# A gated linear-attention kernel on one core: V in three column chunks that carry the router and gate columns, V before K, and a new order of the q stage

## The chip, the cores and the metric

One core of one Trainium2 chip runs the kernel. The metric is device time of one execution in microseconds (us); lower is better. TensorE does the matrix products, VectorE (DVE) and ScalarE (ACT) work on vectors and read the matmul results from PSUM, GpSimd (POOL) works on SBUF alone, and SyncE (SP) issues most transfers. Each engine executes its own queue in order; semaphores order them against each other.

## The reference

The input `x` has 2048 tokens of 1024 numbers (bf16). With 32 heads of 32 columns:

```python
g = sigmoid((x * gate_w).sum(-1, keepdims=True))
q, k, v = heads of x @ wqkv
pq, pk  = q @ w_phi, k @ w_phi                       # per head, 32 x 32
phi     = concat(softmax(p), softmax(-p))            # for q and for k
kv, z   = sum_s phi_k^T v, sum_s phi_k               # per head: 64 x 32 and 64
a       = (phi_q @ kv) / (phi_q . z + 1e-6) @ wo
r       = x @ w_r ; the one token with the largest r goes through a gated FFN (1024 -> 3584 -> 1024)
b       = x + (FFN output * sigmoid(r)) at that token
out     = g * a + (1 - g) * b
```

## The kernel before

**Staging.** The tokens are 16 tiles of 128. `xT_tile(t)` transposes a loaded tile on TensorE into `pT`, and VectorE (even tiles) or ScalarE (odd tiles) copies it to `xT`; it also takes the tile's squared norm on ScalarE (`nx2`, for a range check at the end) and, on VectorE, two products with broadcast rows that give the router value and the gate logit of each token (`rg`). The weights of q and k are folded with `w_phi`: `fold(which, wf, kb)` multiplies a transposed block of `wqkv` (`wT`, loaded by transposing DMAs) with the block-diagonal `BDm`, casts the result on VectorE and takes its squared norm there (`nw2`).

**K and V.** A unit is a tile and a half of the columns (512). `k_v(t, hf)` makes a unit of V with eight matmuls and ScalarE writes it to `v_all`. `k_s0(u)` makes a unit of k features: eight matmuls, two exponentials on ScalarE (`e`), a sum and a reciprocal on VectorE, a product on GpSimd (`phi`). `k_kv(u)`, LAG = 3 iterations behind, adds the products of phi and v into `kvps`, a PSUM region of three banks. The source order is: four tiles' transposes and V, the folds of k with four more tiles, and then one loop that mixes `k_kv`, V units by a running count, `k_s0`, the remaining transposes, the route (`gates_and_route`: the largest router value, its index, the chosen token's column), FFN chunks (1 MB of weights each, two buffers) and the folds of q. The count `nv` starts at 12 when 16 units are done, so units 12 to 15 are made a second time.

**q stage.** `kv_finish` copies kvps to `KV`. `q_front(sb, j)` makes 128 feature columns for 512 tokens (eight matmuls, two exponentials into `E`; 32 in all). `q_num(t, hf)` multiplies a tile's half of the features with `KV` into the PSUM tile `num`, of which there is one buffer; VectorE then runs a chain of seven instructions that ends in `T`, and GpSimd adds the two halves of `T` to `o_sb`. `q_oT(t)` transposes the tile's o by DMA (the last tile on TensorE) and ScalarE makes `xg` from x; `q_wo(t, nh)` multiplies with half of `wo`, VectorE makes the output, SyncE stores it. The loop runs q_num eight iterations behind q_front (NL = 8), q_oT and q_wo two and three behind q_num.

**Order.** A scheduler of the framework takes the program in source order as priority and lets a ready instruction pass one whose inputs or buffer are not there yet by its own reckoning; the order on each engine is then fixed.

**PSUM.** V and K results and q fronts share two buffers (`psA`), transposes, folds and wo results share two others (`psB`).

Of the kernel before, what the change touches and what calls it, by code (L numbers as in the profile page):

```python
# [160 lines left out]
def kernel(  # L161
# [22 lines left out]
    wraw = kscope.enter_context(tc.tile_pool(name="wraw", bufs=2))  # L184
    xs = kscope.enter_context(tc.tile_pool(name="xs", bufs=4))
# [22 lines left out]
    v_all = kpool.tile([P, NU, HH, DH + 1], BF, name="v_all")  # L208
# [36 lines left out]
    wv_sb = wraw.tile([P, KB, D], BF, name="wv_sb", tag="w16")  # L245
    xload(0)
    nc.sync.dma_start(out=wv_sb[:, :, 0:512], in_=w_v[:, :, 2 * D:2 * D + 512])
    for t in range(1, 4):
        xload(t)
    nc.sync.dma_start(out=wv_sb[:, :, 512:D], in_=w_v[:, :, 2 * D + 512:3 * D])  # L250
# [19 lines left out]
    def wT_load(which, kb):  # L270
        if kb == 0:
            wT[which] = wraw.tile([P, KB, D], BF, name="wT", tag="w16")
        nc.sync.dma_start_transpose(out=wT[which][:, :, kb * P:(kb + 1) * P],
                                    in_=A_wqkv[kb * P:(kb + 1) * P, (1 - which) * D:(2 - which) * D])

    def fold(which, wf, kb):
        for jh in range(2):
            pW = psB.tile([P, 4, P], F32, name="pW", tag="pB")
# [8 lines left out]

    def gates_and_route():
# [13 lines left out]
        gw_rows = const.tile([KB, P], BF, name="gw_rows")  # L302
        nc.scalar.dma_start(out=gw_rows[:], in_=gate_w.rearrange("(kb p) -> kb p", p=P))
        gw_ps = m1_ps[:, 0:4].bitcast(BF)
        nc.tensor.transpose(out=gw_ps, in_=gw_rows[:], identity=ident[0:KB, 0:KB])
        nc.vector.tensor_copy(out=gw_sel[:], in_=gw_ps)
# [110 lines left out]
    def k_kv(u):  # L417
        t, hf = divmod(u, 2)
        phi = kst.pop(u)
        for pl in range(NPU):  # L420
# [3 lines left out]
                             rhs=v_all[:, u, 2 * pl:2 * pl + 2, :].rearrange("p h d -> p (h d)"),  # L424
# [104 lines left out]
    for kb in range(KB):  # L529
        wT_load(0, kb)  # L530
    for t in range(4):
        xT_tile(t)
    for t in range(4):
        k_v(t, 0)
    for t in range(4, 8):
        xload(t)
    xT_tile(4)
    for t in range(4):
        k_v(t, 1)
    VL = 12  # L540
    for kb in range(KB):
        fold(0, wkf, kb)
        if kb % 2 == 1:
            xT_tile(5 + kb // 2)
            xload(8 + kb // 2)
# [96 lines left out]
```

## Time and profile before

| | |
|---|---|
| time, median of 3 runs | 354.42 us (353.15 to 354.64) |
| the profiled execution, time | 353.82 us |
| its span, first to last instruction | 352.0 us |
| mean granted TensorE clock | 0.975 of 2.4 GHz |
| busy: TensorE, weight loads, VectorE, ScalarE, GpSimd | 296.9, 161.0, 246.1, 137.4, 115.5 us |
| moved by DMA | 47.98 MB |

Busy time is the sum of an engine's records. A matmul's record also holds the time in which its last results drain while the next one already runs, so the distance between two starts is what a matmul takes of TensorE in a full stretch. Idle time counts only on the path that sets the end.

### The profile page before, as it was taken

The numbers are of one execution on the slowest core, as the hardware profiler recorded it, in microseconds if no ns is written. First come the engines' busy times: TensorE is split into PE (matmuls) and PEld (weight loads), VectorE is DVE, ScalarE is ACT, GpSimd is POOL, SyncE is SP. The second block draws the span as 40 slices with busy tenths as digits, with TensorE's granted clock in tenths as the row PEclk, the third lists the DMA queues.
The fourth block names the chain that finished last, engine by engine and source line by source line (L and its number), as shares of the span: only waits on it lengthen the run. The fifth ranks groups of instructions, "written<-read, shape, count | busy, mean of one in ns | idle before, by whom it ended". The sixth has DMA issues, their size and how long they took to land. (4 is left out here: it accounts for less than half of the span.)

```text
span 352.0 us, 6368 instructions
## 1 busy us (share of the span) xinstructions
PE 296.9 (84%) x2478; PEld 161.0 (46%) x2518; DVE 246.1 (70%) x501; ACT 137.4 (39%) x230; POOL 115.5 (33%) x81
## 2 busy tenths in 40 slices
PE   1398979879779999999998999969999999847590
PEld 0334545435334555655555465535555555423340
DVE  4623999999968435599994237866777777766740
ACT  2434434865524343433343555233343344311110
POOL 5000000355564645456555012331233223321411
PEclk9999999999989999999999999999999999987987
DMA  6999812940000435453465997792344344342201
GB/s 209 281 199 323 289 53 62 177 124 27 2 0 0 122 121 170 149 162 116 128 182 180 312 345 236 211 212 60 92 113 97 91 114 110 89 107 61 60 31 36
DMA packets 64818, 47.98 MB, mean 136 GB/s; under 512 B 35344, under 2 KB 55824, under 8 KB 64784
## 3 DMA queue, kind: packets, MB, share of 16 engines
q1 hardware_dynamic: 63360, 46.94, 47.8%
q10 hardware_dynamic: 1392, 0.59, 0.7%
q8 instruction: 21, 0.34, 0.4%
q14 instruction: 13, 0.11, 0.1%
q0 software_dynamic: 32, 0.00, 0.0%
HBM read 35.19 MB, written 4.20 MB: 112 GB/s over the span
## 5 line engine op out<-in xcount | busy, mean ns | idle before, releaser
L413 POOL TENSOR_TENSOR phi<-e,rs 128x1024 bf16<-128x1024 bf16 x32 | 68.7, 2151 | 114.4 <-DVE rs L411 90.5
L499 POOL TENSOR_TENSOR o_sb<-T 128x512 bf16<-128x512 f32 x32 | 40.6, 1267 | 108.2 <-DVE T L495 108.2
L523 PE MATMUL po<-wo_sb,oT 128*128 128x512 bf16 x249 | 63.0, 394 | 10.7 <-DMA oT<-o_sb 10.3
L391 PE MATMUL pv<-wv_sb,xT 128*128 128x512 bf16 x278 | 69.5, 388 | 0.5
L402 PE MATMUL pk<-wkf,xT 128*128 128x512 bf16 x245 | 62.0, 383 | 0.6
L459 PE MATMUL pq<-xT,wqf 128*128 128x512 bf16 x244 | 59.8, 379 | 0.9 <-ACT E L462 0.3
L265 DVE SCALAR_TENSOR_TENSOR junk<-xs_t,wr_bc 128x1024 bf16<-128x1024 bf16 x32 | 42.8, 1364 | 13.6 <-DMA xs_t<-in_A_x_dram 13.6
L409 DVE TENSOR_REDUCE ssum<-e 128x32 f32<-128x1024 bf16 x32 | 38.7, 1208 | 17.1 <-ACT e L406 17.1
L523 PEld LDWEIGHTS <-oT 128*128 128x128 bf16 x256 | 25.1, 101 | 40.8 <-DMA oT<-o_sb 11.7
L495 DVE TENSOR_TENSOR T<-num,ab 128x1024 f32<-128x1024 f32 x32 | 39.2, 1225 | 3.5 <-DVE ab L493 0.5
L461 ACT ACTIVATE E<-pq 128x512 bf16<-128x512 f32 x32 | 19.1, 596 | 53.0 <-PE pq L459 43.0
L393 ACT CAST v_all<-pv 128x512 bf16<-128x512 f32 x36 | 21.2, 588 | 47.5 <-PE pv L391 47.5
L391 PEld LDWEIGHTS <-xT 128*128 128x128 bf16 x288 | 27.0, 100 | 27.9 <-issue 2.2
L525 DVE SCALAR_TENSOR_TENSOR o_out<-po,gate,xg 128x512 bf16<-128x512 f32 x32 | 23.8, 745 | 22.0 <-PE po L523 22.0
L402 PEld LDWEIGHTS <-xT 128*128 128x128 bf16 x256 | 24.1, 98 | 26.5 <-issue 1.3
L459 PEld LDWEIGHTS <-wqf 128*128 128x128 bf16 x256 | 23.5, 97 | 23.5 <-issue 0.6
L405 ACT ACTIVATE e<-pk 128x512 bf16<-128x512 f32 x32 | 19.1, 598 | 38.7 <-PE pk L402 38.6
L514 ACT ACTIVATE xg<-xin,omg 128x1024 f32<-128x1024 bf16 x16 | 18.4, 1148 | 39.1 <-DVE o_out L525 19.7
L480 PE MATMUL num<-KV,E 128*128 128x136 bf16 x256 | 21.1, 226 | 4.3 <-DVE T L495 4.2
L256 PE MATMUL pT<-ident,xs_t 128*128 128x128 bf16 x128 | 11.3, 242 | 15.2 <-DMA xs_t<-in_A_x_dram 11.7
L480 PEld LDWEIGHTS <-E 128*128 128x128 bf16 x256 | 17.1, 99 | 12.3 <-DVE T L495 7.2
L422 PE MATMUL kvps<-v_all,phi 128*128 128x66 bf16 x256 | 14.0, 194 | 8.9 <-POOL phi L413 8.8
(96 smaller groups left out, 281.0 us busy)
## 6 DMA issues: line engine op xcount, KB each, us to landing
wch<-in_B_w_gate_dram SPq DMA_DIRECT2D x7, 1024.0 KB, 5.3
wch<-in_B_w_up_dram SPq DMA_DIRECT2D x7, 1024.0 KB, 5.5
wchd<-in_B_w_down_dram SPq DMA_DIRECT2D x7, 1024.0 KB, 6.2
xs_t<-in_A_x_dram SPq DMA_DIRECT2D x16, 256.0 KB, 3.9
xin<-in_A_x_dram SPq DMA_DIRECT2D x16, 256.0 KB, 2.7
out_dram<-o_out SPq DMA_DIRECT2D x32, 128.0 KB, 1.9
wv_sb<-in_A_wqkv_dram SPq DMA_DIRECT2D x2, 1024.0 KB, 6.9
wo_sb<-in_A_wo_dram SPq DMA_DIRECT2D x1, 2048.0 KB, 11.4
```

The source lines that it names most:

```text
L265: nc.vector.scalar_tensor_tensor(out=junk2[:], in0=xt_[:], scalar=1.0, in1=wr_bc[:, c, :], op0=ALU.mult, op1=ALU.mult, accum_out=rg[:, c, ...
L391: nc.tensor.matmul(pvf, lhsT=xT[:, kb, t * P:(t + 1) * P], rhs=wv_sb[:, kb, hf * 512:(hf + 1) * 512], start=(kb == 0), stop=(kb == KB - 1))
L393: nc.scalar.copy(out=v_all[:, t * 2 + hf, :, 0:DH], in_=pv[:])
L402: nc.tensor.matmul(pkf, lhsT=xT[:, kb, t * P:(t + 1) * P], rhs=wkf[:, kb, hf * 512:(hf + 1) * 512], start=(kb == 0), stop=(kb == KB - 1))
L409: nc.vector.tensor_reduce(out=ssum[:], in_=e2, axis=AX.X, op=ALU.add)
L413: nc.gpsimd.tensor_tensor(out=phi[:].rearrange("p h s f -> p (h s) f"), in0=e2, in1=_bc(rs[:], [P, HH * 2, DH]), op=ALU.mult)
L459: nc.tensor.matmul(pq[:], lhsT=wqf[:, kb, j * P:(j + 1) * P], rhs=xT[:, kb, sb * SB:(sb + 1) * SB], start=(kb == 0), stop=(kb == KB - 1))
L480: nc.tensor.matmul(num[:, b * NSTR:b * NSTR + KVW], lhsT=E[:, j, sg, tl * P:(tl + 1) * P], rhs=KV[:, sg, j, :], start=True, stop=True)
L495: nc.vector.tensor_tensor(out=T[:].rearrange("p s (j h) d -> p (s j) h d", h=4), in0=nb[:, :, 0:128].rearrange("p b (h d) -> p b h d", d=D ...
L499: nc.gpsimd.tensor_tensor(out=st["o"][:, hf * HH:(hf + 1) * HH, :], in0=T[:, 0], in1=T[:, 1], op=ALU.add)
L523: nc.tensor.matmul(po[:], lhsT=st["oT"][:, kb, :], rhs=wo_sb[:, kb, sl], start=(kb == 0), stop=(kb == KB - 1))
L525: nc.vector.scalar_tensor_tensor(out=o_out[:], in0=po[:], scalar=gate[:, t:t + 1], in1=st["xg"][:, sl], op0=ALU.mult, op1=ALU.add)
```

## The change

V is made in three chunks of columns, 0 to 352, 352 to 704 and 704 to 1026; the last two columns are the router's and the gate's weights, put beside the V weights in SBUF (`rows_in`), so that the matmul gives `rg` and a small VectorE copy takes it out. The two broadcast rows and the products with them are gone. All transposed copies are VectorE's, all squared norms ScalarE's. All of V is made first, each unit once, with all 16 folds among tiles 6 to 15; then all of K, with LAG = 5, 14 FFN chunks, and every fourth phi product on VectorE. In the q stage q_num runs four iterations behind the fronts and takes four tiles' first halves, then their second halves; q_wo takes one half a step, at the earliest three steps behind its q_oT. The chain behind num reads part of its numbers from PSUM instead of from a copy. Buffer counts follow.

```diff
+VC = [0, 352, 704, 1026]
+VW = 1026
...
-    wraw = kscope.enter_context(tc.tile_pool(name="wraw", bufs=2))
-    xs = kscope.enter_context(tc.tile_pool(name="xs", bufs=4))
+    wraw = kscope.enter_context(tc.tile_pool(name="wraw", bufs=1))
+    xs = kscope.enter_context(tc.tile_pool(name="xs", bufs=6))
...
-        nc.scalar.dma_start(out=wr_bc[:, 0, :], in_=B_w_r.unsqueeze(0).to_broadcast([P, D]))
-        nc.scalar.dma_start(out=wr_bc[:, 1, :], in_=gate_w.unsqueeze(0).to_broadcast([P, D]))
+    nc.scalar.dma_start(out=rows[0:KB, :], in_=B_w_r.rearrange("(kb p) -> kb p", p=P))
+    nc.scalar.dma_start(out=rows[KB:2 * KB, :], in_=gate_w.rearrange("(kb p) -> kb p", p=P))
...
+    for c in range(3):
+        lo, hi = VC[c], min(VC[c + 1], D)
+        nc.sync.dma_start(out=wv_sb[:, :, lo:hi], in_=w_v[:, :, 2 * D + lo:2 * D + hi])
+        for t in ((1, 2, 3), (4, 5), ())[c]:
+            xload(t)
+    def rows_in():
+        rows_ps = m2_ps[:, 0:KB].bitcast(BF)
+        nc.tensor.transpose(out=rows_ps, in_=rows[:], identity=ident[0:2 * KB, 0:2 * KB])
+        nc.vector.tensor_copy(out=wv_sb[:, :, D:VW].rearrange("p k c -> p c k"),
+                              in_=rows_ps.rearrange("p (c k) -> p c k", c=2))
+        nc.vector.tensor_copy(out=gw_sel[:], in_=rows_ps[:, KB:2 * KB])
...
-        if t % 2 == 0:
-            nc.vector.tensor_copy(out=xT[:, :, t * P:(t + 1) * P], in_=pT[:])
-        else:
-            nc.scalar.copy(out=xT[:, :, t * P:(t + 1) * P], in_=pT[:])
+        nc.vector.tensor_copy(out=xT[:, :, t * P:(t + 1) * P], in_=pT[:])
+        xsq[t] = xt_
+    def x_norm(t):
...
         nc.scalar.activation(out=junk[:], in_=xt_[:], func=ACTF.Square, accum_out=nx2[:, t:t + 1])
-        for c in range(2):
-            junk2 = wk.tile([P, D], BF, name="junk2", tag="junk", bufs=3)
-            nc.vector.scalar_tensor_tensor(out=junk2[:], in0=xt_[:], scalar=1.0, in1=wr_bc[:, c, :],
-                                           op0=ALU.mult, op1=ALU.mult, accum_out=rg[:, c, t:t + 1])
...
-        if kb == 0:
-            wT[which] = wraw.tile([P, KB, D], BF, name="wT", tag="w16")
+        wT[which, kb] = wraw.tile([P, KB, P], BF, name="wT", tag="wT", bufs=6)
...
-        nc.vector.scalar_tensor_tensor(out=junk3[:], in0=wf[:, kb, :], scalar=1.0, in1=wf[:, kb, :],
-                                       op0=ALU.mult, op1=ALU.mult, accum_out=nw2[:, which, kb:kb + 1])
+        nc.scalar.activation(out=junk3[:], in_=wf[:, kb, :], func=ACTF.Square, accum_out=nw2[:, which, kb:kb + 1])
...
+    def k_v(t, c):
+        lo, hi = VC[c], VC[c + 1]
+        h0, h1 = lo // DH, min(hi, D) // DH
+        pv = psA.tile([P, 512], F32, name="pv", tag="pA")
...
+            nc.tensor.matmul(pv[:, 0:hi - lo], lhsT=xT[:, kb, t * P:(t + 1) * P], rhs=wv_sb[:, kb, lo:hi],
                              start=(kb == 0), stop=(kb == KB - 1))
+        if c == 2:
+            nc.vector.tensor_copy(out=rg[:, :, t], in_=pv[:, D - lo:VW - lo])
...
+        phi = wk.tile([P, HH, 2, DH], BF, name="phi", tag="phi", bufs=6)
+        eng = nc.vector if u % 4 == 3 else nc.gpsimd
+        eng.tensor_tensor(out=phi[:].rearrange("p h s f -> p (h s) f"), in0=e2,
...
+            st = {"o": qw.tile([P, H, DH], BF, name="o_sb", tag="o_sb", bufs=5)}
+            xin = qw.tile([P, D], BF, name="xin", tag="xin", bufs=6)
...
-        nc.vector.tensor_copy(out=ds[:], in_=nb[:, :, 128:136])
+        nc.vector.tensor_copy(out=ds[:], in_=nb[:, 4:8, 128:136])
...
+        nc.vector.tensor_tensor(out=pr[:], in0=nb[:, 0:4, 128:136], in1=ds[:], op=ALU.mult)
...
+    xT_tile(0)
+    rows_in()
+    k_v(0, 0)
+    for t in range(1, 4):
+        xT_tile(t)
+        k_v(t, 0)
+    for t in range(4):
+        k_v(t, 1)
+    xT_tile(4)
+    for t in range(4):
+        k_v(t, 2)
+        x_norm(t)
+        xload(t + 6)
+        wload(1)
+    for t in range(4, NT):
+        if t + 1 < NT:
+            xT_tile(t + 1)
+        if t + 6 < NT:
+            xload(t + 6)
+        if t < 6:
+            wload(1)
+        for c in range(3):
+            k_v(t, c)
+        x_norm(t)
+        for _ in range(0 if t < 6 else 2 if t < 12 else 1):
+            w, kb = fq.pop(0)
+            fold(w, wkf if w == 0 else wqf, kb)
+            wload(1)
+    gates_and_route()
+    LAG = 5
...
     for i in range(NU + LAG):
         if i >= LAG:
             k_kv(i - LAG)
...
+        if i >= 4 and i % 2 == 0 and ci < 14:
             ffn_chunk(ci)
...
-    NL = 8
+    NL = 4
+    WL = 4
...
         if 0 <= n < NU:
-            q_num(n // 2, n % 2)
+            sb, r = divmod(n, 8)
+            q_num(sb * 4 + r % 4, r // 4)
+        m = n - 1
+        if 0 <= m < NU and m % 8 >= 4:
+            t = (m // 8) * 4 + m % 4
+            q_oT(t)
+            wq_ += [(i + WL - 1, t, 0), (i + WL - 1, t, 1)]
...
+        if wq_ and (wq_[0][0] <= i):
+            _, t, nh = wq_.pop(0)
+            q_wo(t, nh)
```

## Rows read from the trace of the kernel before

**Rows 1.** Five stretches: length, busy us and instructions by engine, clock, DMA.

```profile
0.00:34.80 34.80, 19.75 (x105) 10.48 (x108) 15.56 (x27) 12.95 (x20) 5.27 (x16) 1.00 0.95 251
34.80:100.40 65.60, 54.18 (x396) 29.28 (x401) 65.14 (x102) 35.49 (x62) 18.73 (x7) 0.99 0.38 101
100.40:183.30 82.90, 81.01 (x847) 45.56 (x858) 59.31 (x88) 32.46 (x60) 44.36 (x22) 0.99 0.38 116
183.30:301.30 118.00, 111.75 (x973) 61.12 (x987) 77.47 (x215) 49.83 (x81) 34.82 (x26) 1.00 0.60 167
301.30:344.00 42.70, 30.21 (x167) 14.57 (x168) 28.10 (x70) 6.69 (x7) 11.38 (x9) 0.88 0.28 72
```

**Rows 2.** Timeline of TensorE, three stretches: start us, length, line, out<-in.

```profile
39.51 0.61 PE L281 MATMUL pW<-BDm,wT 128*128 128x128 bf16 x8
39.96 1.24 PE L391 MATMUL pv<-wv_sb,xT 128*128 128x512 bf16 x4
...
122.23 0.94 PE L356 MATMUL small_ps<-xsT,wch 128*128 128x1 bf16 x32
123.03 0.41 PE L422 MATMUL kvps<-v_all,phi 128*128 128x66 bf16 x8
123.29 1.89 PE L391 MATMUL pv<-wv_sb,xT 128*128 128x512 bf16 x7
...
251.98 0.64 PE L480 MATMUL num<-KV,E 128*128 128x136 bf16 x8
252.45 1.89 PE L459 MATMUL pq<-xT,wqf 128*128 128x512 bf16 x8
254.18 1.89 PE L523 MATMUL po<-wo_sb,oT 128*128 128x512 bf16 x8
```

**Rows 3.** Timeline of the first 35 us, then one of SyncE's waits.

```profile
5.96 1.31 SPq L242 DMA_DIRECT2D xs_t<-in_A_x_dram  x3
...
6.17 1.03 PE L256 MATMUL pT<-ident,xs_t 128*128 128x128 bf16 x8 [6.17 <-DMA xs_t<-in_A_x_dram]
...
17.45 8.83 PE L391 MATMUL pv<-wv_sb,xT 128*128 128x512 bf16 x32
...
31.50 0.58 SPq L575 DMA_DIRECT2D wo_sb<-in_A_wo_dram  x1
...
SPq L242 <- DMA wr_bc<-in_B_w_r_dram: 4.2, 1, 4.2
```

**Rows 4.** Groups of instructions by line: count, busy us, mean ns, idle before.

```profile
L413 POOL TENSOR_TENSOR phi<-e,rs 128x1024 bf16<-128x1024 bf16 x32 | 68.7, 2151 | 114.4 <-DVE rs L411 90.5 <-PE kvps L422 5.1 <-ACT v_all L393 4.9
L523 PE MATMUL po<-wo_sb,oT 128*128 128x512 bf16 x249 | 63.0, 394 | 10.7 <-DMA oT<-o_sb 10.3
...
L265 DVE SCALAR_TENSOR_TENSOR junk<-xs_t,wr_bc 128x1024 bf16<-128x1024 bf16 x32 | 42.8, 1364 | 13.6 <-DMA xs_t<-in_A_x_dram 13.6
...
L409 DVE TENSOR_REDUCE ssum<-e 128x32 f32<-128x1024 bf16 x32 | 38.7, 1208 | 17.1 <-ACT e L406 17.1
...
L393 ACT CAST v_all<-pv 128x512 bf16<-128x512 f32 x36 | 21.2, 588 | 47.5 <-PE pv L391 47.5
...
L262 ACT ACTIVATE junk<-xs_t 128x1024 bf16<-128x1024 bf16 x16 | 17.0, 1061 | 5.8 <-DMA gw_rows<-in_gate_w_dram 4.3 <-DMA xs_t<-in_A_x_dram 1.5
...
L283 DVE CAST wqf<-pW 128x512 bf16<-128x512 f32 x16 | 10.5, 671 | 2.6 <-PE pW L281 2.6
...
L262 ACT ACTIVATION_READ_ACCUMULATOR junk<-xs_t 128x1 f32 x16 | 3.1, 194 | 0.0
```

**Rows 5.** Timeline of TensorE behind the last q matmul.

```profile
316.75 1.11 PE L480 MATMUL num<-KV,E 128*128 128x136 bf16 x8
...
321.88 0.64 PE L480 MATMUL num<-KV,E 128*128 128x136 bf16 x8
...
329.73 0.65 PE L480 MATMUL num<-KV,E 128*128 128x136 bf16 x8 [0.67 <-DVE T L495]
333.25 0.65 PE L480 MATMUL num<-KV,E 128*128 128x136 bf16 x8 [2.87 <-DVE T L495]
```

More of the change, by code (lines that the diff above doesn't have):

```diff
@@ L207 @@
     wkf = kpool.tile([P, KB, D], BF, name="wkf")
-    v_all = kpool.tile([P, NU, HH, DH + 1], BF, name="v_all")
+    v_all = kpool.tile([P, NT, H, DH + 1], BF, name="v_all")
     KV = big.tile([P, 2, KB, KVW], BF, name="KV")
@@ L243, in xload @@
         xtiles[t] = xt_
-    wv_sb = wraw.tile([P, KB, D], BF, name="wv_sb", tag="w16")
+    wv_sb = wraw.tile([P, KB, VW], BF, name="wv_sb", tag="w16")
     xload(0)
[L247 to L250, printed above, removed]
+    for c in range(3):
[9 more added lines that the diff above has]
+        nc.vector.tensor_copy(out=gw_sel[:], in_=rows_ps[:, KB:2 * KB])
     def xT_tile(t):
@@ L301, in gates_and_route @@
         nc.sync.dma_start(out=r_row[0:1, :], in_=rT[:])
[L302 to L306, printed above, removed]
         mx8 = const.tile([1, 8], F32, name="mx8")
@@ L385, in moe_final @@
                             in_=y2[:], accum_op=ALU.add)
-    def k_v(t, hf):
-        pv = psA.tile([P, HH, DH], F32, name="pv", tag="pA")
-        pvf = pv[:].rearrange("p h f -> p (h f)")
+    def k_v(t, c):
+        lo, hi = VC[c], VC[c + 1]
+        h0, h1 = lo // DH, min(hi, D) // DH
+        pv = psA.tile([P, 512], F32, name="pv", tag="pA")
         for kb in range(KB):
-            nc.tensor.matmul(pvf, lhsT=xT[:, kb, t * P:(t + 1) * P], rhs=wv_sb[:, kb, hf * 512:(hf + 1) * 512],
+            nc.tensor.matmul(pv[:, 0:hi - lo], lhsT=xT[:, kb, t * P:(t + 1) * P], rhs=wv_sb[:, kb, lo:hi],
                              start=(kb == 0), stop=(kb == KB - 1))
-        nc.scalar.copy(out=v_all[:, t * 2 + hf, :, 0:DH], in_=pv[:])
+        nc.scalar.copy(out=v_all[:, t, h0:h1, 0:DH], in_=pv[:, 0:(h1 - h0) * DH].rearrange("p (h d) -> p h d", d=DH))
+        if c == 2:
+            nc.vector.tensor_copy(out=rg[:, :, t], in_=pv[:, D - lo:VW - lo])
     kst = {}
@@ L423, in k_kv @@
                              lhsT=phi[:, 2 * pl:2 * pl + 2, :, :].rearrange("p h s f -> p (h s f)"),
[L424 removed]
+                             rhs=v_all[:, t, hf * HH + 2 * pl:hf * HH + 2 * pl + 2, :].rearrange("p h d -> p (h d)"),
                              start=False, stop=(t == NT - 1), skip_group_check=True)
@@ L527, in q_wo, with wload @@
         nc.sync.dma_start(out=out2[t * P:(t + 1) * P, sl], in_=o_out[:])
-    for kb in range(KB):
-        wT_load(0, kb)
-    for t in range(4):
[L532 to L536, printed above, removed]
+    wq = [(0, kb) for kb in range(KB)] + [(1, kb) for kb in range(KB)]
+    fq = list(wq)
+    def wload(n):
+        for _ in range(n):
+            if wq:
+                wT_load(*wq.pop(0))
+    xT_tile(0)
[4 more added lines that the diff above has]
+        k_v(t, 0)
+    for t in range(4):
+        k_v(t, 1)
     xT_tile(4)
     for t in range(4):
[L539 to L545, printed above, removed]
-        if 8 + kb // 2 < VL and kb % 2 == 1:
-            for hf in range(2):
-                k_v(4 + kb // 2, hf)
-    LAG = 3
+        k_v(t, 2)
[18 more added lines that the diff above has]
+    LAG = 5
     ci = 0
-    nv = 12
-    nx = 9
-    nq = 0
     for i in range(NU + LAG):
@@ L557 @@
             k_kv(i - LAG)
-        want = min(NU, 12 + (i + 1) * (NU - 12) // 26)
-        while nv < want:
-            k_v(nv // 2, nv % 2)
-            nv += 1
         if i < NU:
             k_s0(i)
-        if nx < NT and i % 1 == 0:
-            xT_tile(nx)
-            if nx + 3 < NT:
-                xload(nx + 3)
-            nx += 1
-            if nx == NT:
-                gates_and_route()
-        if i >= 12 and i % 2 == 0 and ci < 13:
+        if i >= 4 and i % 2 == 0 and ci < 14:
             ffn_chunk(ci)
             ci += 1
-        if i == 27:
+        if i == 20:
             nc.sync.dma_start(out=wo_sb[:], in_=A_wo.rearrange("(kb p) n -> p kb n", p=P))
-        if i >= 8 and nq < KB:
-            wT_load(1, nq)
-            nq += 1
-        if 20 <= i < 20 + KB:
-            fold(1, wqf, i - 20)
-        if i == 30:
+        if i == 28:
             range_flag()
@@ L589 @@
     n_front = NSB * KB
-    NL = 8
-    for i in range(n_front + NL + 4):
+    NL = 4
+    WL = 4
+    wq_ = []
+    i = 0
+    while i < n_front + NL + 2 or wq_:
         n = i - NL
         if 0 <= n < NU:
-            q_num(n // 2, n % 2)
-        m = n - 2
-        if 0 <= m and m % 2 == 0 and m // 2 < NT:
-            q_oT(m // 2)
+            sb, r = divmod(n, 8)
[5 more added lines that the diff above has]
+            wq_ += [(i + WL - 1, t, 0), (i + WL - 1, t, 1)]
         if i < n_front:
             q_front(i // KB, i % KB)
-        m = n - 3
-        if 0 <= m < NU:
-            q_wo(m // 2, m % 2)
+        if wq_ and (wq_[0][0] <= i):
+            _, t, nh = wq_.pop(0)
+            q_wo(t, nh)
         if i % 2 == 1 and ci < 21:
```

24 lines of the change are left out of this document (11 added, 13 removed).

## The prediction

> **What bounds the kernel now.** I read the stretches first [rows 1], cut where the work changes: at 34.8 us the first weight fold starts, at 183.3 the first q matmul, at 301.3 the q matmuls are over, at 344 all matmuls. TensorE looks busy everywhere but at the ends, but a matmul's record includes its drain, so I priced the work by the distance between starts in full stretches [rows 2]. Eight matmuls of 512 columns: 252.45 to 254.18, 1.73 us, one "unit". Eight num matmuls 0.47, a gate or up chunk 0.80, eight kv products 0.26, a fold or a tile of transposes (eight of 128 columns) 0.45.
>
> The program asks for 36 V units, 32 K, 32 q and 32 wo (132 x 1.73 = 228.4), 16 transposed tiles and 16 folds (14.4), 32 kv (8.3), 32 num (15.0), 21 chunks (16.8) and about 1 of small things: 284 of the 352 us. So TensorE's own work is the floor and 68 us are lost. Stage by stage (units by the code's order and the counts in the rows):
> - 0 to 34.8: eight V units and five transposed tiles, 16.1; lost 18.7. The first V matmul starts at 17.45, since the code transposes four tiles before it; SyncE issued the second x load only at 5.96, after 4.2 us of waiting for the first broadcast row [rows 3].
> - 34.8 to 183.3: 28 V, 32 K, 27 folds and transposes, 29 kv, 10 chunks: 132; lost 16.5. Up to 100.4 the reason is VectorE, busy 65.1 of 65.6 us; behind it TensorE is nearly full [rows 1].
> - 183.3 to 301.3: 111 of work, 7 lost.
> - 301.3 to 344: the 167 matmuls are 8 num groups, 12 wo halves and one transposed tile, 25; lost 17.7. With no q work left, wo waits for the DMA that transposes o (10.3 us in all [rows 4]), num groups for the one PSUM buffer (329.73 to 333.25, idle 2.87 behind DVE T [rows 5]), and the granted clock falls to 0.88 of the 2.4 GHz level in the mean [rows 1].
> - The end, from 344 to 352, 8.0: last output, last accumulate, exit.
>
> **The change, part by part.**
>
> V work. Before runs 36 V units where 32 are needed (VL stops at tile 7, but nv starts again at 12, so units 12 to 15 run twice; 36 evictions [rows 4]): -6.9. Three chunks of 352, 352 and 322 columns cost, by columns, 1.19 + 1.19 + 1.09 = 3.47 against 3.46 for two units. A third more weight loads ride along: num changes weights every 136 columns at 59 ns a matmul [rows 2], so loads can't bind at 322. Work: 284 - 6.8 = 277.
>
> Start. V needs one transposed tile and 0.7 MB of weights before its first matmul instead of four tiles and 1 MB, and the two 256 KB broadcasts are gone. Where the second x load waited for a broadcast, a 2 KB row load now stands. x0 was there at 6.17 before [rows 3]; the added transpose of the two rows and its copies fit ahead of the first weight chunk. I expect the first V matmul at 8, some at half clock, and the four tiles' V done at 24 if the chunks land in the order issued. 3.6 MB of x and weights at the stage's 251 GB/s [rows 1] are 14 us, plus a wait for the slow w_phi loads: third chunk at about 18. Lost here 8 instead of 18.7; bounds 6 (loads hidden) and 13 (each chunk late by one).
>
> V stage, tiles 4 to 15. Work 12 x 3.47 + 11 x 0.45 + 16 x 0.45 = 54. VectorE loses the router and gate products (42.8 us [rows 4]) and the folds' squares (16 of the same form, so 21.8), and takes all transposed copies and a small copy of the two new columns, which stands ahead of that tile's casts and so holds chunk 2's PSUM buffer no longer than ScalarE does: nothing. In a tile with two folds it has four casts at 0.67, a copy like them and the small one: 3.6 of the tile's 4.8 us of matmuls. ScalarE gets three evictions (a 512-column one is 588 ns; between 404, by columns, and 588; I take 450), one x square and two fold squares at 1.06 plus what isn't overlapped of 0.19, about 1.15 [rows 4]: 4.8. That is as much as TensorE. The squares stand in ScalarE's queue ahead of the next tile's first eviction; TensorE can fill two PSUM buffers and then waits: chunk 2's eviction, three squares and one eviction are 4.4 us, against 3.75 of folds, transposes and two chunks. So about 1 us a tile for the six two-fold tiles; the other six have one or none and room. Also x loads from the seventh on wait for a square (its tile's release), and the 4 MB of gate weights and wo issued as soon as SyncE is free (wo at 31.50 [rows 3]) may stand ahead of them: 0 to 8 us, once. Queued behind such a wait on SyncE are the transposing loads, six tiles ahead of their folds. Lost: 8, bounds 3 and 18.
>
> K stage. All V is done, so nothing covers latencies but K: per step 1.73 + 0.26 + half a chunk 0.35 to 0.40 = 2.4 us, against two 0.6 exponentials on ScalarE, on VectorE 1.21 for the sums, about 0.3 for the reciprocal and a quarter of a phi product, on GpSimd three quarters of 2.15 [rows 4]. The phi product on VectorE isn't in the trace; the nearest rows are its two-input product, 1.36, and the same phi product on GpSimd, 2.15: 0.34 to 0.54 a step, so VectorE stays under 2.1; I take nothing, and 0.5 us a step in the first steps, where no chunk runs yet, goes into the upper bound. The route chain (transpose, DMA, max, index, a register) now starts with K; before it was spread over 29 us. If TensorE's order puts the gate's matmul too early it waits. Before lost 3.4 from 100.4 on (79.5 of work in 82.9); I take 6, bounds 3 and 12.
>
> q stage and tail. Four q fronts instead of eight cover the last kv and its copies: 3.5 lost (0 to 8). num now takes four tiles' first halves, then the second, so it starts four steps after the fronts and leaves four groups behind the last front instead of eight; o's transpose has three steps until wo reads it. Behind the last front stand 4 num, 12 wo halves, one tile: 23. num groups follow each other at 3.5 without cover (329.73 to 333.25) and up to 5.1 (316.75 to 321.88) [rows 5]; 32 of them at 3.5 to 3.9 are 112 to 125, below the stage's 132 of TensorE work, but near. Reading part of num from PSUM instead of ds keeps seven instructions in the chain; I cost it at nothing: the chain is covered while fronts or wo remain, and bare it is worth a tenth of a microsecond either way. Lost in the stage and tail 8 beside the handoff, 11.5 in all instead of 25; bounds 7 and 25. The end stays 8.
>
> Sum: 277 + 8 + 8 + 6 + 11.5 + 8 = 318.5 span, and the profiled execution is 1.8 over its span (353.82 against 352.0): 320 us. The median before is 354.42, 0.6 over the profiled one, so about 10% faster.
>
> **A rule against the change.** The rows say that a square over 1024 bf16 costs ScalarE 1.06 and 0.19, and the product of that size VectorE 1.36 [rows 4]. The Trainium skill, ScalarE: Activation LUTs, section Rules for kernel authors, says to do multiplications and the like on VectorE, which is up to about three times faster per element in bf16. By that a square here would cost ScalarE up to 4.1 us, a two-fold tile 13.6 instead of 5, and the time would be some 370; the row of the very same square in this kernel speaks against it.
>
> **The rivals.**
> 1. *ScalarE binds V.* Tiles pay for every square in turn, because evictions queue behind them: 6.4 us for a two-fold tile, 5 for a one-fold one, and x loads, which wait for squares, come late too. V loses 20 instead of 8: 332. For it: ScalarE and TensorE are equal on paper. Against it: only six tiles carry two folds.
> 2. *num binds q.* One PSUM buffer, groups at 3.9 to 4.1 as in the tail before, plus 10 us to start and 6 behind the last: 146 instead of 132 + 11.5, and if the tail's cold steps return, 152: 322 to 330. For it: the tail [rows 5]. Against it: from 183.3 to 301.3 num kept up.
> 3. *Slower.* Every num step costs what the one from 316.75 to 321.88 did, 5.1 us, since four o transposes in a row hold SyncE's queue, and with it the stores behind them that free the output buffers: 32 x 5.1 + 16 = 179, 36 more than the forecast's 143.5, 356. It decides from 5.1 a step. Against it: that step ran at the lower clock.
> 4. *VectorE wasn't the reason before 100.4*, and the stage's 13 lost come from loads; then only start, units and tail gain: 333.
>
> **How the numbers follow.** Forecast (306 to 330) 0.66, first rival 0.14, second beyond 330 0.06, fourth 0.06, slower by the third rival 0.04 and by the squares of the rule 0.01, another 0.03 above 342, most of it within half a percent of before. All low bounds: 277 + 6 + 3 + 3 + 7 + 8 + 1.8 = 306; all high ones 355. The range, 306 to 342, takes in the first, second and fourth rivals and leaves out less than 0.2. Half a percent, 1.8 us, is what a measurement here can tell; faster by more 0.93, same 0.02, slower 0.05.
>
> **What would show it.** Right: 48 evictions of V; first V matmul by 9 us and the first four tiles' V done by 25; VectorE below 80% up to the end of V, which comes at 83 to 90 us; 14 chunks in K; first num some 10 us after the last K matmul; under 30 us from the last q matmul to the last wo. Wrong: gaps of several us of TensorE behind v_all (ScalarE) or x loads in V; more than 10 us of TensorE idle behind the route chain; num steps over 4.1 us while fronts remain.

## The result and the profile after

The changed kernel takes 318.45 us (median of 4 runs, 317.62 to 319.27) against 353.78 us before: a ratio of 0.9005, 95% interval 0.896 to 0.9051. The forecast was 320.0. The profiled execution took 317.62 us, 1.9 more than its span of 315.7.

The stretches of the kernel after, as in [rows 1], cut where the work changes: four tiles' V, the other V with all folds, K, q up to the last q matmul, the tail up to the last wo matmul, the end.

```profile
0.00:26.90 26.90, 19.88 (x137) 13.42 (x138) 5.99 (x14) 13.58 (x26) 5.29 (x16) 1.00 1.05 266
26.90:82.80 55.90, 55.78 (x506) 39.84 (x504) 27.72 (x53) 38.91 (x83) 0.00 (x0) 1.00 0.52 138
82.80:160.90 78.10, 76.01 (x959) 44.25 (x957) 65.48 (x95) 36.40 (x72) 43.78 (x23) 1.00 0.57 180
160.90:270.80 109.90, 107.60 (x863) 57.56 (x860) 78.44 (x221) 47.34 (x79) 33.61 (x26) 1.00 0.51 145
270.80:307.70 36.90, 28.89 (x161) 14.54 (x160) 22.93 (x56) 7.79 (x8) 8.86 (x7) 0.91 0.24 65
307.70:315.70 8.00, 0.40 (x2) 0.00 (x0) 0.75 (x1) 0.00 (x0) 0.96 (x1) 0.67 0.13 36
```

VectorE, full from 34.8 to 100.4 us before (65.14 of 65.60), is half busy in the V stage (27.72 of 55.90), and TensorE has no idle time there. What is left is in the tail, at clock 0.91, and at both ends. With the prediction's unit prices the work in the six stretches is 16.1, 53.8, 74.9, 106.6, 25.9 and 0: 277.3. The counts are those of the trace and the prices those of the prediction, so the sum tests the counts, not the prices. The rest of each stretch is lost time:

| lost, us | before | forecast | after |
|---|---|---|---|
| start (first four tiles' V) | 18.7 | 8 | 10.8 |
| rest of V, and K | 16.5 | 8 + 6 | 2.1 + 3.2 |
| q, and tail | 7.1 + 17.7 | 11.5 | 3.3 + 11.0 |
| end | 8.0 | 8 | 8.0 |
| sum | 68 | 41.5 | 38.4 |

Groups by line, after: count, busy us, mean ns, idle before.

```profile
L418 POOL TENSOR_TENSOR phi<-e,rs 128x1024 bf16<-128x1024 bf16 x24 | 45.7, 1912 | 111.1 <-DVE rs L415 98.9 <-DVE cc L324 4.4 <-DVE bb L341 3.8
...
L395 ACT CAST v_all<-pv 128x352 bf16<-128x352 f32 (+1 forms) x48 | 20.8, 438 | 15.5 <-PE pv L393 15.5
...
L274 ACT ACTIVATE junk<-xs_t 128x1024 bf16<-128x1024 bf16 x16 | 16.9, 1056 | 3.2 <-DMA xs_t<-in_A_x_dram 3.2
...
L418 DVE TENSOR_TENSOR phi<-e,rs 128x1024 bf16<-128x1024 bf16 x8 | 12.0, 1503 | 0.5
...
L292 ACT ACTIVATE junk<-wkf 128x1024 bf16<-128x1024 bf16 x8 | 8.5, 1057 | 3.9 <-DVE wkf L290 3.9
```

The products of 1.36 us each with the broadcast rows [rows 4] are gone; the moved squares (L292) cost ScalarE what those of x do; V has 48 evictions, and they wait for matmuls (15.5 us), not matmuls for them, but for one wait of 0.59 us in the start. Two rows were not to be had before: the phi product on VectorE, 1.50 us (0.38 a step; I had 0.34 to 0.54), and the one on GpSimd in this kernel, 1.91. The 2.15 of before is a mean: 2.68 for the seven between 60 and 100 us, where VectorE was full, and 1.92 to 2.10 later.

TensorE's timeline, after: the start, then one tile of the V stage that carries two folds (the last row is the next tile's).

```profile
3.73 1.03 PE L267 MATMUL pT<-ident,xs_t 128*128 128x128 bf16 x8 [3.73 <-DMA xs_t<-in_A_x_dram]
...
7.63 1.03 PE L267 MATMUL pT<-ident,xs_t 128*128 128x128 bf16 x8 [2.52 <-DMA xs_t<-in_A_x_dram]
8.45 4.90 PE L393 MATMUL pv<-wv_sb,xT 128*128 128x352 bf16 x16
13.15 1.20 PE L267 MATMUL pT<-ident,xs_t 128*128 128x128 bf16 x16
14.94 7.32 PE L393 MATMUL pv<-wv_sb,xT 128*128 128x352 bf16 x48 [0.59 <-ACT v_all L395]
...
51.38 0.61 PE L267 MATMUL pT<-ident,xs_t 128*128 128x128 bf16 x8
51.82 2.15 PE L393 MATMUL pv<-wv_sb,xT 128*128 128x352 bf16 x14
...
56.51 0.61 PE L267 MATMUL pT<-ident,xs_t 128*128 128x128 bf16 x8
```

The first V matmul starts at 8.45, but after one 2.52 us wait for the second x tile, which stands ahead of it in TensorE's queue. The first 16 matmuls then take 4.70 us, 0.294 each; the 48 from 14.94 take 7.16, 0.149 each. A tile with two folds takes 5.13 us and holds no idle row. ScalarE's timeline shows what the row at 14.94 waits for:

```profile
12.36 1.06 ACT L274 ACTIVATE junk<-xs_t 128x1024 bf16<-128x1024 bf16 x1 [1.53 <-DMA xs_t<-in_A_x_dram]
...
14.46 0.78 ACT L395 CAST v_all<-pv 128x352 bf16<-128x352 f32 x2
```

Six squares of x stand in ScalarE's queue ahead of the first two evictions, and the fifth waits 1.53 us for its x tile.

TensorE's timeline behind the last q matmul, answering to [rows 5], and the stretch at the lower clock:

```profile
279.53 0.64 PE L485 MATMUL num<-KV,E 128*128 128x136 bf16 x8
...
283.36 0.65 PE L485 MATMUL num<-KV,E 128*128 128x136 bf16 x8 [1.96 <-DVE T L500]
287.96 0.61 PE L528 MATMUL po<-wo_sb,oT 128*128 128x512 bf16 x1 [3.95 <-DMA oT<-o_sb]
288.37 1.11 PE L485 MATMUL num<-KV,E 128*128 128x136 bf16 x8
...
292.26 1.11 PE L485 MATMUL num<-KV,E 128*128 128x136 bf16 x8
293.36 1.89 PE L528 MATMUL po<-wo_sb,oT 128*128 128x512 bf16 x8
297.34 0.40 PE L516 MATMUL oT_ps<-ident,o_sb 128*128 128x128 bf16 x4 [2.09 <-POOL o_sb L504]
297.58 10.52 PE L528 MATMUL po<-wo_sb,oT 128*128 128x512 bf16 x48
```

```profile
288.37:293.36 4.99, 4.99 (x24) 2.86 (x23) 3.04 (x8) 0.00 (x0) 1.23 (x1) 0.50 0.28 53
```

The three idle rows are 8.0 us. From 288.37 to 293.36 two num groups and seven wo matmuls, worth 2 x 0.47 + 7 x 0.216 = 2.45, take 4.99 at the lower clock level (0.50 of 2.4 GHz): 2.5 lost. Together 10.5 of the tail's 11.0. The last of the waits is odd: behind it stand 48 wo matmuls, and only the last tile's 16 need the transposes that wait.

### The profile page after: what moved, and what is told of

It is laid out like the page before. It is cut to its first block, busy times and chain, and to the rows that moved or that the text cites. A ratio compares the mean times of both kernels' runs of the same rounds, so it can differ in the third digit from the quotient of the medians.

```text
span 315.7 us, 6529 instructions
## 1 busy us (share of the span) xinstructions
PE 288.6 (91%) x2614; PEld 169.6 (54%) x2614; DVE 201.3 (64%) x438; ACT 144.0 (46%) x266; POOL 92.5 (29%) x73
## 5 line engine op out<-in xcount | busy, mean ns | idle before, releaser
L418 POOL TENSOR_TENSOR phi<-e,rs 128x1024 bf16<-128x1024 bf16 x24 | 45.7, 1912 | 111.1 <-DVE rs L415 98.9
L528 PE MATMUL po<-wo_sb,oT 128*128 128x512 bf16 x256 | 64.2, 387 | 4.0 <-DMA oT<-o_sb 4.0
L393 PE MATMUL pv<-wv_sb,xT 128*128 128x352 bf16 (+1 forms) x384 | 63.9, 315 | 0.7 <-ACT v_all L395 0.6
L406 PE MATMUL pk<-wkf,xT 128*128 128x512 bf16 x256 | 60.6, 379 | 1.0 <-ACT e L410 1.0
L464 PE MATMUL pq<-xT,wqf 128*128 128x512 bf16 x256 | 61.1, 379 | 0.3 <-ACT E L467 0.3
L393 PEld LDWEIGHTS <-xT 128*128 128x128 bf16 x384 | 36.7, 99 | 17.4 <-DVE xT L268 0.5
L409 ACT ACTIVATE e<-pk 128x512 bf16<-128x512 f32 x32 | 19.1, 597 | 39.9 <-PE pk L406 22.0
L406 PEld LDWEIGHTS <-xT 128*128 128x128 bf16 x256 | 22.9, 97 | 23.8 <-issue 1.1
L395 ACT CAST v_all<-pv 128x352 bf16<-128x352 f32 (+1 forms) x48 | 20.8, 438 | 15.5 <-PE pv L393 15.5
L489 DVE COPY ds<-num 128x32 f32<-128x32 f32 x32 | 6.1, 192 | 25.4 <-PE num L485 25.3
L268 DVE COPY xT<-pT 128x1024 bf16<-128x1024 bf16 x16 | 10.9, 688 | 17.2 <-PE pT L267 16.6
L410 ACT ACTIVATE e<-pk 128x512 bf16<-128x512 f32 x32 | 18.9, 591 | 0.0
```

The lines of the kernel that those rows point to most:

```text
L393: nc.tensor.matmul(pv[:, 0:hi - lo], lhsT=xT[:, kb, t * P:(t + 1) * P], rhs=wv_sb[:, kb, lo:hi], start=(kb == 0), stop=(kb == KB - 1))
L395: nc.scalar.copy(out=v_all[:, t, h0:h1, 0:DH], in_=pv[:, 0:(h1 - h0) * DH].rearrange("p (h d) -> p h d", d=DH))
L406: nc.tensor.matmul(pkf, lhsT=xT[:, kb, t * P:(t + 1) * P], rhs=wkf[:, kb, hf * 512:(hf + 1) * 512], start=(kb == 0), stop=(kb == KB - 1))
L409: nc.scalar.activation(out=e[:, :, 0, :], in_=pk[:], func=ACTF.Exp)
L418: eng.tensor_tensor(out=phi[:].rearrange("p h s f -> p (h s) f"), in0=e2, in1=_bc(rs[:], [P, HH * 2, DH]), op=ALU.mult)
L464: nc.tensor.matmul(pq[:], lhsT=wqf[:, kb, j * P:(j + 1) * P], rhs=xT[:, kb, sb * SB:(sb + 1) * SB], start=(kb == 0), stop=(kb == KB - 1))
```

## Experiments

The theory after the result: VectorE was the bound up to 100.4 us before, its relief is the largest part of the gain, and the q order is the second. The rivals: the gain came from the double V units or from the loads at the start; ScalarE is now the bound of V. For the tail: TensorE's fixed order holds ready wo matmuls behind waits; the rival was that the latencies themselves must be made shorter.

**VectorE's load put back (e3).** The fold squares go back to VectorE, and two products of x with itself for each tile, which nothing reads, stand for the old ones with the broadcast rows. For their space `wT` has 5 buffers instead of 6.

```diff
+            nc.vector.scalar_tensor_tensor(out=junk2[:], in0=xt_[:], scalar=1.0, in1=xt_[:],
+                                           op0=ALU.mult, op1=ALU.mult, accum_out=rgx[:, c, t:t + 1])
...
-        nc.scalar.activation(out=junk3[:], in_=wf[:, kb, :], func=ACTF.Square, accum_out=nw2[:, which, kb:kb + 1])
+        nc.vector.scalar_tensor_tensor(out=junk3[:], in0=wf[:, kb, :], scalar=1.0, in1=wf[:, kb, :],
+                                       op0=ALU.mult, op1=ALU.mult, accum_out=nw2[:, which, kb:kb + 1])
```

> The changed kernel with VectorE given back the work that it lost in the V stage: the folds' squares on VectorE, and two products of 1024 bf16 a tile (of x with itself, result unused; one transposed weight buffer less to make room). If VectorE was the bound up to 100 us before, the V stage's VectorE time grows from 27.7 to about 77 us over 55.9 us of stage, and the whole takes 338 to 343. If the 13 us lost there came from loads, it stays within 3 us of 318.5.

329.57 us (328.09 to 330.17), ratio 0.932 (0.9279 to 0.9361): 11 us more than the changed kernel. Its start, the rest of V, and K:

```profile
0.00:31.50 31.50, 20.77 (x144) 13.95 (x145) 26.63 (x49) 13.80 (x26) 5.28 (x16) 1.00 0.96 268
31.50:90.90 59.40, 55.93 (x499) 39.90 (x497) 58.18 (x110) 24.79 (x54) 0.00 (x0) 1.00 0.45 108
90.90:173.40 82.50, 79.01 (x959) 45.05 (x957) 66.07 (x101) 34.98 (x70) 44.51 (x23) 0.96 0.54 170
```

VectorE is full again (58.18 of 59.40) and V ends 8.1 us later. Up to there TensorE waits 7.8 us for VectorE's copies (`xT`, `rg`, `wkf`), where the changed kernel has no such wait; the smaller `wT` is not the reason, since e8 has it too and loses nothing. The cause stands; the size was less than the 338 to 343 expected, since VectorE's work up to the end of V rose by 51 us (26.63 and 58.18, against 5.99 and 27.72) and its spare time of 20.9 us in the start and 28.2 in V took in most of it. K is 4.4 longer as well, at clock 0.96, so not all of the 11 us is VectorE's load in V.

**The fold squares alone (e4).** The second hunk of e3 by itself.

> The changed kernel with only the folds' squares back on VectorE (x's squares stay on ScalarE). If what counts is that VectorE is below TensorE in the V stage (27.7 + 21 of 55.9 us), nothing changes: 317.5 to 319.5. If evictions queued behind squares on ScalarE still cost something, it gains up to the 2 us that V loses. If the page's rule on VectorE against ScalarE held, it would gain tens of us.

321.08 us (320.96 to 321.65), ratio 0.9093 (0.9061 to 0.9126): 2.6 more, which none of the three expectations had. The V stage and K, and TensorE's timeline in K:

```profile
26.90:83.00 56.10, 55.26 (x503) 39.79 (x501) 43.62 (x85) 25.14 (x55) 0.00 (x0) 1.00 0.53 136
83.00:163.90 80.90, 77.34 (x958) 44.38 (x956) 64.93 (x96) 35.14 (x69) 44.50 (x23) 0.98 0.56 175
```

```profile
98.17 0.34 PE L317 MATMUL small_ps<-gw_sel,xsT 128*1 128x1 bf16 x8 [1.06 <-DVE xsT L315]
100.47 1.67 PE L407 MATMUL pk<-wkf,xT 128*128 128x512 bf16 x7 [0.74 <-ACT e L411]
...
104.06 0.43 PE L428 MATMUL kvps<-v_all,phi 128*128 128x66 bf16 x8 [1.49 <-POOL phi L419]
...
105.95 3.32 PE L407 MATMUL pk<-wkf,xT 128*128 128x512 bf16 x8
```

The V stage, with 13.8 us taken off ScalarE and 15.9 put on VectorE, ends at 83.0 instead of 82.8: neither engine binds it, so ScalarE as the bound of V (rival 1) is out, and so is a gain from ScalarE's squares as such. The 2.6 are lost in K, behind three gaps of 0.74 to 1.49 us; the eight matmuls from 105.95 then take 3.32 instead of the usual 1.89, at clock 0.52. The first gap is the route's: its matmul waits for VectorE's copy `xsT`, for which the changed kernel's TensorE did not wait.

**The double units: taken out of before (e1), put into after (e11).** In e1 the count starts where it should; in e11 the V of tiles 6 and 7 is made twice.

```diff
-    nv = 12
+    nv = 16
```

> The kernel before with one number changed: the running count of V units starts at 16, so that units 12 to 15 are made once. Theory of the prediction: TensorE's work is the floor and four units of 1.73 us are 6.9 us of it, so 354 becomes 347. Rival: these four units ran at 60 to 80 us, where VectorE was the bound, and cost nothing there; then the time stays at 353 to 354 and the 6.9 us count only once VectorE is relieved.

349.51 us (347.51 to 352.68), ratio 0.9914 (0.9872 to 0.9957). By the ratio that is 3.0 us, by the medians of the runs taken together (353.53 before) 4.0, of the 6.9 us of matmuls; the first q matmul comes 3.3 earlier (180.1).

```diff
-        for c in range(3):
+        for c in (0, 1, 2, 0, 1, 2) if t in (6, 7) else (0, 1, 2):
```

> The changed kernel with V of tiles 6 and 7 made twice: the kernel before did these four units twice, and to make them once there gained 3.0 us. With VectorE relieved TensorE's work should set the time of the V stage, and two tiles' V are 2 x 3.47 us: 325.4. If V has slack on TensorE still, it takes 320 to 322.

324.97 us (324.76 to 327.62), ratio 0.9218 (0.9149 to 0.9287): 6.5 more for 6.9 of matmuls, as expected; K starts at 89.6 instead of 82.8. So the same matmuls cost their price where TensorE is full, and about half of it (1.5 to 4.5 by the interval) where VectorE was full. The start of this run, which its edit leaves alone, is of use below:

```profile
8.33 3.83 PE L393 MATMUL pv<-wv_sb,xT 128*128 128x352 bf16 x16
...
14.83 7.32 PE L393 MATMUL pv<-wv_sb,xT 128*128 128x352 bf16 x48 [1.79 <-ACT v_all L395]
```

**The broadcasts put back (e7).** Two 256 KB row broadcasts, which nothing reads, are issued first on ScalarE's queue.

```diff
+        nc.scalar.dma_start(out=wqf[:, 0, :], in_=B_w_r.unsqueeze(0).to_broadcast([P, D]))
+        nc.scalar.dma_start(out=wqf[:, 1, :], in_=gate_w.unsqueeze(0).to_broadcast([P, D]))
```

> The changed kernel with the two broadcast rows of 256 KB loaded again, ahead of the two small row loads (into a tile that is overwritten later, nothing reads them). If the second x load waits for the first broadcast as it did before, the first V matmul slides from 8.45 to about 10 to 12 us and the time to 321 to 324. If the start is set by the arrival of x0 and the first weight chunk, it moves by less than 1.5 us.

321.5 us (321.35 to 323.64), ratio 0.9088 (0.9033 to 0.9144): 3 more. The start, all engines:

```profile
1.84 6.08 SPq L247 DMA_DIRECT2D xs_t<-in_A_x_dram  x3
...
11.86 0.50 PE L395 MATMUL pv<-wv_sb,xT 128*128 128x352 bf16 x1
```

The three x loads need 6.08 us to issue instead of 3.33, V starts 3.4 later, K 3.5 later. Of the 7.9 us that the start gained, about 3 are the broadcasts; the rest is put down to the order in which V begins, which was not tried alone.

**The old q order (e2).** The q loop of the kernel before, on the changed kernel.

```diff
-    NL = 4
-    WL = 4
-    wq_ = []
-    i = 0
-    while i < n_front + NL + 2 or wq_:
+    NL = 8
+    for i in range(n_front + NL + 4):
...
-            sb, r = divmod(n, 8)
-            q_num(sb * 4 + r % 4, r // 4)
+            q_num(n // 2, n % 2)
```

> The changed kernel with the q loop of before: num eight steps behind the fronts, tile by tile, o's transpose and wo two and three steps behind num. If the new order of the q stage is worth what the ledger says (25 us lost from the first q matmul to the last one before, 14.3 after), this takes 329. If the tail's loss is set by the one num buffer whatever the order, it stays within 2 us of 318.5.

326.7 us (325.48 to 327.58), ratio 0.925 (0.9208 to 0.9292): the new order is worth 8.2 us, where 10.5 were expected. From the first q matmul, at 160.9 in both, to the last wo are 155.3 us instead of 146.8, and TensorE waits 13.3 us for the DMAs that transpose o instead of 4.0.

**A wait in K (e8).** ScalarE's exponentials wait 9.8 us in all for phi products on GpSimd that still read `e`; a fourth buffer of `e` takes the wait away (`wT` 5 buffers for the space).

```diff
-        e = wk.tile([P, HH, 2, DH], BF, name="e", tag="e")
+        e = wk.tile([P, HH, 2, DH], BF, name="e", tag="e", bufs=4)
```

> The changed kernel with four instead of three buffers for the k exponentials (and five instead of six for the transposed weights). In the first 25 us of K VectorE's max and index push the sums back, and ScalarE waits 9.8 us for the phi product to free an e buffer; TensorE loses 3.2 us in K. If these buffers are the wait, it gains 1 to 3 us (316 to 317.5); if the route chain itself is, nothing changes.

317.33 us (316.96 to 319.77), ratio 0.8971 (0.8914 to 0.9028), not to be told from the change. The wait falls to 1.2 us and K is 77.8 instead of 78.1: it was off the path.

**The tail: shorter latency (e5).** The o of the last four tiles is transposed on TensorE instead of by DMA.

```diff
-        if t < NT - 1:
+        if t < NT - 4:
```

> The changed kernel with o of the last four tiles (12 to 15) transposed on TensorE and copied by ScalarE; before this only tile 15. If the 11 us lost behind the last q matmul come from the DMA that transposes o (idle 3.95 us, and the half clock behind it), this takes 312 to 316. If num's chain sets the tail, wo waits as long for o itself and it stays at 317 to 320.

322.23 us (321.71 to 322.63), ratio 0.9094 (0.9044 to 0.9144): 3 to 4 slower, where 312 to 316, or 320 at most, was expected. Its TensorE timeline:

```profile
282.84 1.09 PE L485 MATMUL num<-KV,E 128*128 128x136 bf16 x8 [2.25 <-DVE T L500]
...
285.88 3.15 PE L528 MATMUL po<-wo_sb,oT 128*128 128x512 bf16 x7 [1.10 <-ACT oT L517]
...
294.23 0.62 PE L516 MATMUL oT_ps<-ident,o_sb 128*128 128x128 bf16 x8 [0.72 <-POOL o_sb L504]
```

The 3.95 us wait for the DMA is gone, and waits for GpSimd's sum and for ScalarE's copy stand at each of the four tiles instead: each transpose in TensorE's queue is one more place where what is behind it waits. The idle rows of the tail sum to 8.4 us, no less than the 8.0, and TensorE is busy 31.7 us in it instead of 28.9, of which the three tiles' transposes are 1.35 (3 x 0.45).

**Slower wo (e6), no transposes (e12), both (e9, e10).** e6 spends three wo halves in four steps while fronts remain, so that more are left for the tail, with buffers to match.

```diff
-        oT = qw.tile([P, KB, P], BF, name="oT", tag="oT", bufs=3)
+        oT = qw.tile([P, KB, P], BF, name="oT", tag="oT", bufs=6)
...
-        if wq_ and (wq_[0][0] <= i):
+        if wq_ and (wq_[0][0] <= i) and (i % 4 != 3 or i >= n_front):
```

> The changed kernel with wo held back: one half in three of four steps instead of in every step while there are fronts, with more buffers for o, its transpose and x. It does the same work; num and the fronts run ahead of wo, and more wo is left to cover the last num chain. If TensorE ran out of wo because num stood one step of 3.93 us apart from the next, this takes 309 to 315. If the tail is bound by the chain of num alone (3.5 us each, one buffer), it gains under 2 us, and it loses if the fronts become the wait.

316.34 us (314.48 to 317.89), ratio 0.8926 (0.8864 to 0.8989): 2 less, short of the 309 to 315 expected, and its interval overlaps the changed kernel's. The end of its TensorE timeline shows why:

```profile
289.64 0.40 PE L516 MATMUL oT_ps<-ident,o_sb 128*128 128x128 bf16 x4 [2.09 <-POOL o_sb L504]
289.88 15.70 PE L528 MATMUL po<-wo_sb,oT 128*128 128x512 bf16 x70
```

70 wo matmuls, kept to fill such waits, stand behind the one for the last tile's transposes, which only 16 of them need. The Trainium skill, TensorE: Matmul & The Clock Gate, section Step-by-step: what each phase is for, says that matmuls keep program order and only weight loads are pulled ahead; the row agrees.

e12 takes the transposes out of the queue, alone:

```diff
-        if t < NT - 1:
+        if t < NT:
```

> The changed kernel with one edit: o of the last token tile is transposed by a DMA as the others' are, not by eight transposes on TensorE; the share of wo chunks in the q loop and all buffers are as in the changed kernel. It splits the 9 us that the version with this edit and slower wo together had. Theory in-order block: the eight transposes stand between the last num and 50 to 70 wo matmuls that could run, and TensorE takes its instructions in order; without them the 2.09 us idle at 297 and the transposes' own time (about 0.6 us) go, and the time is 315 to 316.5. Rival, pacing is the whole of it: with most wo chunks spent before the last q there is nothing left to cover the last six num groups, the idle stretches before them stay or move behind the last num as a wait for the DMA of the last tile (about 2 us issue to landing), and the time stays at 317.5 to 319.5.

315.5 us (315.06 to 318.62), ratio 0.8947 (0.8871 to 0.9023), span 313.2 instead of 315.7, as the theory of the queue's order had it, though this interval overlaps the changed kernel's too. Its tail:

```profile
283.57 0.65 PE L485 MATMUL num<-KV,E 128*128 128x136 bf16 x8 [2.19 <-DVE T L500]
288.09 0.61 PE L528 MATMUL po<-wo_sb,oT 128*128 128x512 bf16 x1 [3.87 <-DMA oT<-o_sb]
...
294.15 11.46 PE L528 MATMUL po<-wo_sb,oT 128*128 128x512 bf16 x49
```

The last wait is gone and the wo matmuls run through; the other two, and the lower clock behind them, stay. e9 joins both edits and e8's buffers:

```diff
-        if t < NT - 1:
+        if t < NT:
...
-        if wq_ and (wq_[0][0] <= i):
+        if wq_ and (wq_[0][0] <= i) and (i % 4 != 3 or i >= n_front):
```

> The changed kernel with wo paced at three in four steps, four buffers for the k exponentials, and o of tile 15 transposed by DMA like the others, so that no transpose stands in TensorE's queue ahead of wo that is ready (idle 2.09 us and 70 matmuls behind it in the paced run). If the tail is in-order waiting plus too little wo left, this takes 311 to 314. If num's chain (3.3 us a step bare) is the whole of it, it stays at the paced run's 316.

309.35 us (308.33 to 310.91), ratio 0.8761 (0.8713 to 0.8809): better than the 311 to 314 expected, and clear of the changed kernel. Its tail:

```profile
266.52 0.65 PE L485 MATMUL num<-KV,E 128*128 128x136 bf16 x8 [0.22 <-DVE T L500]
267.00 3.40 PE L528 MATMUL po<-wo_sb,oT 128*128 128x512 bf16 x15
270.46 0.64 PE L485 MATMUL num<-KV,E 128*128 128x136 bf16 x8
...
284.08 3.19 PE L528 MATMUL po<-wo_sb,oT 128*128 128x512 bf16 x14 [0.78 <-DMA oT<-o_sb]
```

Between the num groups now stand 16 wo matmuls, 3.46 us, about as much as the chain behind num needs (bare steps of 3.28 in e5). The idle rows sum to 1.0 instead of 8.0 and the clock column stays at 1.00. By the spans of the profiled executions the single edits give 2.5 (e12), 2.4 (e6) and 0.3 (e8), 5.2 in all, and together 9.2: the work kept back is of use only where nothing stands in front of it, and the cover also takes the lower clock away. e10 spends two halves in three steps, with `oT` and `xin` buffers to match.

```diff
-        if wq_ and (wq_[0][0] <= i):
+        if wq_ and (wq_[0][0] <= i) and (i % 3 != 2 or i >= n_front):
```

> As the run before, with wo paced at two in three steps and more buffers. Fronts, num and two thirds of wo are 3.35 us of TensorE a step, about the bare chain of num (3.3), so num can't run further ahead than this. Theory: another 1 us or none, 310 to 314; if num's chain falls behind the fronts TensorE idles in the middle instead and it takes 314 to 318.

308.22 us (307.0 to 309.35), ratio 0.8728 (0.8681 to 0.8775), below the 310 to 314 expected. No idle row is left in its tail. It is the fastest version of the study, 10 us below the change, though not to be told from e9 with certainty.

## Why the prediction was right, and where it was off

**The mechanism was right for V and for the q order, less so for the start and the tail.** VectorE was the reason before 100.4 us, so rival 4 is out (e3: 11 us for as many products and squares as it had). TensorE's work came out as forecast, 277.3 against 277. Lost time fell by 11.2 us in V and K, by 7.9 in the start, by 10.5 in q and tail. Put back one at a time, VectorE's load costs 11.1, the q order 8.2, the double units 6.5 and the broadcasts 3.0: 28.8 of the 35.3 us between the medians; no run assigns the rest. The nearness of 318.45 to 320 owes something to terms that erred in opposite directions:

- *V tiles, 8 lost, low bound 3:* 2.1, below the bound. The step that failed is ScalarE's 4.8 us for a two-fold tile and, from it, the full us a tile. It was busy 4.25 of 5.13: evictions took 0.44, of which a part overlaps the next instruction, and squares followed each other more closely than the 1.15 I took. TensorE's order put the folds between the chunks' matmuls; that this gave both engines time is read from the rows, not tried. No wait is left, and V ends at 82.8, just ahead of the 83 to 90 given. A two-fold tile costs 0.3 more than its price (5.13 for 4.82), six of them nearly all of the 2.1.
- *Start, 8:* 10.8, within its bounds. First V at 8.45, as forecast; four tiles done at 26.9, not 24 or 25. What held V behind 8.45 was not in the forecast of this stage: ScalarE's order, which has six x squares and a wait for an x tile ahead of the first evictions. It is the first rival's mechanism, evictions queued behind squares, in the start instead of in V. The half rate of the first 16 matmuls, 2.3 us by itself (4.70 less 16 x 0.149), cost next to nothing: in e11 the same 16 took 3.66, and the 48 behind them began at 14.83 instead of 14.94, since they wait for the same evictions.
- *K, 6:* 3.2, near the low bound. No row has TensorE waiting for the route chain (in e4 one has, 1.06 us), and the wait for `e` did not count (e8). 14 chunks, as listed.
- *q and tail, 11.5:* 14.3. Listed as a sign, "under 30 us from the last q matmul to the last wo" was wrong: 36.9. I counted by the source four num groups behind the last front; in TensorE's order there are six. And "the chain is covered while fronts or wo remain" took remaining work for reachable work: wo remained, but in order behind a wait. The shorter `ds`, put at a tenth of a microsecond for a bare step, may be worth a little more: bare steps are 3.28 in e5 and were 3.52 before, in another order of work. First num came 12.9 us after K, forecast 10. The 146.8 us of q and tail are the 146 of rival 2, and the num steps while fronts remained, 3.93, lie in its 3.9 to 4.1; but that is chance. A step of 3.93 is 0.47 and 16 wo or q matmuls of TensorE's own work, which left 3.3 us idle or lost in the whole stage, and in e10, with less wo in a step, num groups mostly follow each other at 3.3 while fronts remain. So num did not bind, and the 5.1 us steps of rival 3 did not appear either.
- *The double units, 6.9:* the price in the sum is right, since it was taken as TensorE's work with the lost time apart. As an edit alone it is worth 3.0 to 4.0 in the kernel before (e1) and 6.5 in the one after (e11).

**The rule against the change** would have given some 370. The rows show the square at 1.06 us on ScalarE in its new place too, and with the fold squares on VectorE the kernel is 2.6 slower, not faster (e4). The Trainium skill, ScalarE: Activation LUTs, section Rules for kernel authors, gives its factor of up to about three for operations with a single source. The product that stands for a square on VectorE names two, and took 1.22 us in e4 against 1.06 and 0.19 on ScalarE: so the forecast's reading carried the factor to a form that the Trainium skill does not name there, and no run here tried one with a single source. For a square of 1024 with a sum the two engines are near each other.

**Left open.** Why the first 16 matmuls ran at half rate stays open. That ScalarE's order sets the start, and what sets e4's lost time in K going, was read from the traces and not tried; a run with the x squares behind the first evictions would be the test. LAG, the chunks in K, the phi products on VectorE and the shorter `ds` were not changed alone. The ends (8 us) were not touched.

## What to carry to other kernels

Price TensorE by start-to-start distances and keep its lost time apart, stage by stage: then the same edit is seen to be worth its full price in a full stage and about half of it under another engine's bound. Work kept back to cover a tail helps only if nothing that waits stands ahead of it in the engine's own order; read that order from the trace, not from the loop. A faster way to make a late operand is a loss if it adds waiting places to the busy queue, as the four tiles' transposes did. The same holds for ScalarE in the start: squares that nothing waits for stood ahead of the evictions that TensorE waited for.

## What was not expected of the hardware

- TensorE drops to the lower clock level behind rather short gaps in the tail: after idle rows of 1.96 and 3.95 us it ran at 0.50 from 288.37 to 293.36, and with gaps of at most 0.78 (e9) it stayed at 1.00.
- The first 16 V matmuls, of 352 columns, are 0.294 us apart, twice the 0.149 of those behind them, as at the lower clock level, while the granted clock of that stretch reads 1.00. In e11 they are 0.229 apart in the mean, with the same kernel up to there:

```profile
8.45:13.15 4.70, 4.70 (x19) 2.42 (x18) 0.69 (x1) 3.17 (x7) 0.00 (x0) 1.00 1.11 335
```

- A V unit broken off for folds costs more than both apart. Four V matmuls of 352 columns between folds take 0.72 us: their starts are 0.15 apart, as in a row, but from the last of them to the fold behind it are 0.26 to 0.27. Two such breaks and a smaller one (0.23) are the 0.3 us that a two-fold tile costs over its price.
